# Interleaving the V rows by four over the partitions in a fused sketch-attention and feed-forward kernel, with a new hand-written order of work

## The chip, the core and the metric

One core of a Trainium2 chip runs the whole kernel. The metric is the device time of one launch in microseconds, as the median of repeated runs. A profiled execution gives, beside its own time, the span from its first to its last instruction and what each engine did in it.

The engines are named as the profile names them: PE (matrix multiply; PEld is its weight load), DVE (vector), ACT (activation functions), POOL (general vector work) and SP (which here only issues DMAs). An issue row, such as `SPq`, is the engine's sequencer starting a DMA. PSUM is the memory that PE writes, SBUF the memory that everything else works in, with 128 partitions.

## The reference

Four batches (b), four heads (h), 1088 positions (s), head size 32, sketch size 8. All tensors are float32.

```python
def phi(x):                                   # 32 -> 64 features
    a = np.einsum('rd,bhsd->bhsr', S1, x)
    b = np.einsum('rd,bhsd->bhsr', S2, x)
    return np.einsum('bhsi,bhsj->bhsij', a, b).reshape(*x.shape[:-1], r * r)
q_p, k_p = phi(q), phi(k)
kv = np.einsum('bhsf,bhsd->bhfd', k_p, v)
z = np.sum(k_p, axis=2)
num = np.einsum('bhsf,bhfd->bhsd', q_p, kv)
den = np.einsum('bhsf,bhf->bhs', q_p, z)[..., None] + 1e-06
x = (num / den).transpose(0, 2, 1, 3).reshape(4352, 128)
h = x @ w_in                                  # 128 -> 2048
out = (h * (1.0 / (1.0 + np.exp(-h)))) @ w_out   # 2048 -> 128
```

The sums over keys (`kv` and `z`) run over all 1088 positions in any order, so the key and value rows may be dealt to partitions and columns in any way, as long as a key and its value meet in the same partition of the same block of 128.

## The kernel before, in words

**Two halves.** The attention half works batch by batch. For each batch a key part makes `kv` and `z`, and a query part makes the 128 x 1088 block `xT` (features by tokens). The feed-forward half then takes `xT` in pieces of 256 or 512 tokens: `h` steps (L729, PE, w_in times x into a PSUM tile of two banks), SiLU (L733, ACT, 128x1024 elements at a time) and `o` steps (L746 or L743, PE, the sum over the 2048 hidden columns). There are 68 SiLU instructions: 16 for the whole tokens of each batch, and 4 for the tokens left over by all batches (two of each 34 per partition, task `mR`). A piece ends with a copy or transpose to an output tile `ot` (L751 on DVE, L164 or L162 for the last ones) and four stores (L701, L707, L712). The H tiles in PSUM are two, so an `h` step waits until the SiLU two steps back has read its tile. Output tiles come from a pool of 3.

**Key part of one batch** (`key_tasks`, from L294). A key or value of a head is position 34 i + a, with i from 0 to 31 and a from 0 to 33. The 34 values of a are cut into four groups c with `KA = [0, 9, 18, 26, 34]`, sizes `KN = [9, 9, 8, 8]`.
- `kt` (L301, L304): DVE transposes K in 32 x 32 blocks into `KT`, two groups c at a time. Group c goes to `KT[:, c, :]`, as 9 or 8 blocks of 32 consecutive columns. For batch 0 it is four instructions (two for each of the two parts of the load), for each later batch two, of 576 and 512 columns.
- `proj` (L268 to L274): PE, both sketches of the keys. `tr` (L321): DVE transposes the sketches back to `kab`, keys over the partitions: partition 32 c + i holds what group c has for i.
- `outer` (L324 to L327): DVE or POOL makes the 64 features per key and head, `kp`. `z` (L329), `l2`, `wm`: the denominators' weights.
- `load_v` (L188): V of group c goes to partitions 32 c to 32 c + 31, one DMA per group, 128 to 144 KB. `vcast` (L401) makes bfloat16 of it on ACT, POOL or DVE. `kv0` (batch 0, L357) and `kv` (L379): PE sums kp times V over the keys, nine blocks of 128 (the last of 64). `kvm`, `kvt`, `kvc`: copies and a transpose of the result.

**Query part.** Batch 0 (`query_tasks`, from L532) works in small spans so that the first tokens come soon: `tr` (L543, DVE), `proj`, `projm` (L558), `back` (L565), `backm` (L570), `scale` (L473 to L476), `outer` (L481), a transpose on PE (`pet`, L502) and a copy (`petc`), `num` (L515), and the copy `x` to `xT`. Batches 1 to 3 (`query_tasks_hm`, from L605) work in one piece: `tr` (L613, L615), `proj` (L621, which takes one of the two H tiles until `back1` has read it), `back` 0 to 3 (L633, L634), `scale` (L641 to L644), `outer` 0 to 2 (L649), a DMA transpose for each outer (L655), `num` (L661, L669), and `x0`, `x1`, which copy halves of `xT`. Both copies must be done before the batch's first `h` step.

**What sets the order.** Every instruction is a task with a number, in order of creation; `ORDER` (L16) is a hand-written list of these numbers, and every engine executes its tasks in that order, strictly one after the other. After the point, `74` or `2.1` names the engine where a task may run on several. `Plan.replay` (L85) goes through the list once with costs written in the code, only to deal out buffers and to decide how many filler matmuls on zeros (L872) stand between the first PE tasks; the filler count is fixed when the program is built.

The orders of the queues around the change, read from `ORDER` (`m02` is the piece of batch 0 whose tokens begin at block 2, `m14` that of batch 1 at block 4, and so on):

```
DVE  k0kt00 k0kt20 WP WB4 k0kt05 k0tr00 k0kt25 k0tr10 k0outer0 k0tr05 k0tr15 q0tr4 q0tr0 k0outer6 q0back14
     k0wm q0back10 q0back04 q0back00 q0backm00 q0backm20 q0scale20 q0outer20 q0scale00 k1kt00 k1kt20 q0backm44
     q0scale44 k1tr00 k1tr10 q0x0 q1tr q0petc4 q0petc6 k2kt00 k2kt20 q1back0 q1back1 q1back3 q1back2 q1scale
     q1outer1 q1outer0 k1outer6 k2tr00 k2tr10 q2tr k1kvm m00tr k1kvc k3kt20 k2wm q1x0 k3kt00 q2back0 ...
POOL k0outer1 k0outer3 k0outer7 k0outer5 k0vcast5 q0outer00 cwi1 cwi2 q0outer44 q0outer64 WQ k1outer8 k1outer0
     cwo0 cwo1 k1outer4 cwo3 cwi3 k1vcast k1outer2 k2outer2 q1outer2 ...
ACT  lv03 lv02 l2out lv12 k0zt k0vcast0 k0kvm q0petc2 cwi0 q0x2 lv13 q0petc0 m02s0 m02s1 ... m04s7 q1x1 m14s0 ...
PE   ... k0proj0 l2in k0proj5 k0z q0proj4 k0l2 q0proj0 q0projm0 q0projm4 k0kv0 ... k0kv3 q0pet2 q0num2 q0pet0
     m02h0 k1proj m02h1 ... m04h5 k1kv k2z m04h6 k1kvt m04h7 k2l2 q1num m04o4 m04o5 q2proj m14h0 m04o6 m04o7
     m10h0 m02o0 m10h1 k3proj q1numr m14h1 m02o1 m14h2 m02o2 m10h2 m02o3 ...
SP   lqb lqa lv00 lv01 lk1 lwi0 lwi1 lq1 lk2 lwo0 lwo1 lwo2 lv11 lwo3 lk3 lv10 lq2 q1dmat1 q1dmat0 ...
```

Names: `lk`, `lq`, `lv` are loads of K, Q and V (`lqa` and `lqb` the two parts of batch 0's Q, of 256 and 288 KB; `lv03` is group 3 of batch 0), `lwi` and `lwo` the weights' loads, `cwi` and `cwo` their casts. Batch 0's K is loaded by four DMAs on SP ahead of all this (L203 to L205). The S1 and S2 loads and four of the sixteen V loads (`lv02`, `lv03`, `lv12`, `lv13`) are issued by ACT.

Of the kernel before, what the change touches and what calls it, by code (L numbers as in the profile page):

```python
# [16 lines left out]
0 74 7 25 28 22 1 24 29 23 2.1 97 3.1 30 33 8 5 31 11 34 6 102 32 100 35 38.1 140 40.0 36 14 37 75  # L17
16 50 42.0 18 55 51 99 76 20 52 46.1 56 79 48.0 53 59 57 78 58 77 44.0 60 26.0 67 27.1 68 39 41
69.0 47 45 49 61 43 70 54.1 104 71.0 62.1 9.1 105 72 10.0 73.0 80 63 183 81 101 12.0 241 98 64.0
106 145 242 244 82.1 107 65 108 245 247 66.1 87.1 114 122 248 226 83 4 115 88 113.0 227 84.1 116  # L20
229 109.0 89.1 117.1 147 85 230 123 15.0 148 90 86.0 124 17.0 232 91.0 125 228 111.0 233 127 231
126 256 19.1 128 259 257 149 21.0 234 260 13.0 262 131.0 258 263 235 261 129.0 236 132 265 264
103.0 266 112.1 268 130 237 150 269 110.0 250 151 267 165 251 271 153.0 118 272 157 119.0 133.1 274
238 158 156.0 120 277 239 275 121.0 191 159 155.0 135 240 160.0 278 270 137.1 273 190 138.0 134 166
310 167 188 276 168 311 144 279 170 142 283 280 143 243 284 286 169 282 192 171 287 136 313 281 246
314 316 187 193 249 172.1 141 317 289 185 252 290 312 253 292 194 254 285 176.0 293 319 174.0 288
255 146.0 320 322 152.1 315 175 323 295 139.1 154.1 291 296 196.0 298 173 200 299 301 197.0 184 294
201 186 302 325 92.1 177 202 161 326 328 162.0 203.0 297 329 163 304 164.0 208 300 305 178 189.0
# [91 lines left out]
def kernel(  # L120
# [31 lines left out]
    op = ctx.enter_context(tc.tile_pool(name="op", bufs=3))  # L152
# [35 lines left out]
    def load_v(eng, b, c):  # L188
        n = KN[c]
        eng.dma_start(  # L190
            Vx[b][32 * c: 32 * (c + 1), :, 0:n].rearrange("p h a d -> p h (a d)"),
            AP(tensor=v.tensor, offset=v[b, 0].offset + KA[c] * D,
               ap=[[SA * D, 32], [S * D, H], [1, n * D]]))
# [46 lines left out]
    for t in KTs:  # L240
        nc.vector.memset(t[:, 2:4, NB * 32:], 0.0)
    for t in Vf:
        nc.vector.memset(t[64:, :, NB, :], 0.0)
# [21 lines left out]
    def dma(kb, fn, deps=(), issue=0.47, lag=1.8, due=None, ready=0.0, eng="SP", rate=300.0, name=""):  # L265
        return pl.add(eng, issue, fn, deps, lag=lag, due=due, ready=ready, dq=kb / rate, name=name)
# [9 lines left out]
    def load(b):  # L276
# [8 lines left out]
        if b >= 2:  # L285
# [4 lines left out]
        ks[b]["lv"] = [dma(139, lambda c=c: load_v(nc.scalar if b == 1 and c > 1 else nc.sync, b, c), dv, due=at + 0.5, rate=220.0,  # L290
                           eng="ACT" if b == 1 and c > 1 else "SP", name=f"lv{b}{c}") for c in range(4)]
        qs[b]["lq"] = dma(557, lq, dq, due=at + 1.0, name=f"lq{b}")

    def key_tasks(b, cuts):  # L294
# [6 lines left out]
        def kt(c, lo, hi):  # L301
            hi = min(hi, KN[c])
            src = Kx[b][:, KA[c]: KA[c + 2], :].rearrange("p (c a) d -> p c a d", c=2)[:, :, lo:hi, :]
            nc.vector.transpose(out=KT[:, c:c + 2, 32 * lo: 32 * hi], in_=src.rearrange("p c a d -> p c (a d)"))  # L304
# [24 lines left out]
        def z(sl):  # L329
            st["z"] = sl  # L330
            for t in range(NBX):
                n, c = (P if t < NB else XN), t % 4
                nc.tensor.matmul(sl[32 * c: 32 * (c + 1), 0:HR], st["ab"][:n, 1, t, :], st["ab"][:n, 0, t, :],  # L333
# [23 lines left out]
        def kv0(lo, hi):  # L357
            i = st.get("n", 0)
            kpf = st["kp"].rearrange("p (t q g) i j -> p t q (g i j)", q=2, g=2)
            for t in range(lo, hi):  # L360
                m = P if t < NB else XN
                for p in range(2):
                    nc.tensor.matmul(H0[:, p, 0:64].rearrange("p (g d) -> p g d", g=2), kpf[:m, t, p, :],
                                     Vb[b][:m, 2 * p: 2 * p + 2, t, :], start=(i == 0), stop=(i == NBX - 1))
                i += 1
# [13 lines left out]
        def kv(sl):  # L379
            st["kvp"] = sl  # L380
            kpf = st["kp"].rearrange("p (t h) i j -> p t h (i j)", h=H)
            for t in range(NBX):
                n = P if t < NB else XN
                for h in range(H):
                    nc.tensor.matmul(sl[D * h: D * (h + 1), 0: R * R], Vb[b][:n, h, t, :],
                                     kpf[:n, t, h, :], start=(t == 0), stop=(t == NB),
# [18 lines left out]
        if b == 0:  # L405
            lv = [dma(139, lambda c=c: load_v(nc.scalar if c > 1 else nc.sync, 0, c), due=5.0 + 0.1 * c, rate=230.0,
                      eng="ACT" if c > 1 else "SP", name=f"lv0{c}") for c in range(4)]
# [415 lines left out]
    ld_qa = dma(262, lambda: load_x(nc.sync, Qx[0], q, 0, 0, 16), due=4.0, rate=250.0, name="lqa")  # L823
# [81 lines left out]
```

## Time and profile before

| what | value |
|---|---|
| median of 11 runs | 99.05 us (97.02 to 101.03) |
| the profiled execution's own time | 98.15 us |
| its span, first to last instruction | 96.3 us |
| busy in the span: PE, ACT, DVE, POOL | 87.1, 72.4, 56.8, 31.6 us |
| of PE's busy time, fillers on zeros | 9.9 us (54 matmuls) |
| SiLU on ACT | 64.8 us, 68 instructions |
| first `h` step on PE | 17.48 us after the span's start |
| batch 1's first `h` step | 37.09 us |
| last `o` step ends | about 91.4 us |
| packets of DMA | 28506, 12.93 MB |

How to read it. Times in the profile count from the start of the span. In a row of the timeline the first number is the start, the second the busy time of the instructions that the row merges; the note in brackets is the engine's idle time ahead of it and what ended it. In a row of the table by stretches the engines' busy times stand in order, with their instruction counts, then the clock granted to PE, the mean busy share of 16 DMA engines and the GB/s moved. PE is busy in nine tenths of the span, but a good part of that is fillers and waiting matmuls, and its busy time is modelled at the ends of instructions; what is late at a given place is read from the row at that place.

### The profile page before, as it was taken

Reading aid. Unit: us, or ns where it says so; the run is one execution under the profiler, and the core shown is the slowest. Engines: PE = TensorE matmul, PEld = TensorE weight load, DVE = VectorE, ACT = ScalarE, POOL = GpSimd, SP = SyncE. Lnnn points to the kernel's source line nnn. Section 1 sums busy time; section 2 is a strip of 40 time slices with the busy share of each in tenths; the row PEclk is TensorE's granted clock in tenths of the full one; section 3 lists DMA queues with packets and bytes.
Section 4 is the critical chain, followed back from the end, with each engine's and each line's share of the span. In section 5 each row is a group of like instructions: output and inputs, shape, how many; then the busy total and the mean of one; then the engine's idle time right before and its main releaser. Section 6 shows DMA issues by size and latency. Waiting matters only on the chain.

```text
span 96.3 us, 2487 instructions
## 1 busy us (share of the span) xinstructions
PE 87.1 (90%) x962; PEld 51.9 (54%) x972; DVE 56.8 (59%) x153; ACT 72.4 (75%) x89; POOL 31.6 (33%) x46
## 2 busy tenths in 40 slices
PE   5999599989999789999999999999999999999900
PEld 4645359776566434465454344544565854579800
DVE  4665879599999998948607394999207022020210
ACT  3310115899999884799999689999999989999700
POOL 5019605799881390061194450053000000000000
PEclk9999859999999999999999999999999999999999
DMA  1989999999700843299878100671740433406220
GB/s 39 251 252 241 328 349 396 371 241 269 216 22 7 162 74 68 65 298 195 187 151 186 33 0 0 101 117 34 137 85 0 70 72 61 76 0 95 47 63 14
DMA packets 28506, 12.93 MB, mean 134 GB/s; under 512 B 23120, under 2 KB 26704, under 8 KB 28496
## 3 DMA queue, kind: packets, MB, share of 16 engines
q1 hardware_dynamic: 27680, 12.20, 52.8%
q10 hardware_dynamic: 816, 0.60, 2.6%
q8 instruction: 7, 0.11, 0.6%
q14 instruction: 3, 0.02, 0.1%
HBM read 8.79 MB, written 2.23 MB: 114 GB/s over the span
## 4 chain that ended last, share of the span: by engine, by line
PE 66%; DMA 15%; DVE 8%; SPq 5%; issue 2%; DVEq 0%
PE H L729 26%; PE B L746 22%; DMA Qx<-in_q_dram 7%; DMA qt<-qp 4%; PE B L872 4%; DMA out_dram<-ot 4%; SPq L701 2%; SPq L186 2%; PE B L743 2%; DVE kab L321 2%; PE B L272 1%; DVE qp L649 1%; PE H L621 1%; DVE QT L613 1%; PE B L558 1%
## 5 line engine op out<-in xcount | busy, mean ns | idle before, releaser
L733 ACT ACTIVATE G<-H 128x1024 bf16<-128x1024 f32 x68 | 64.8, 1034 | 5.3 <-PE B L621 2.3
L729 PE MATMUL H<-xT,w_in 128*128 128x512 bf16 (+1 forms) x153 | 36.9, 336 | 0.1
L746 PE MATMUL B<-G,w_out 128*128 128x512 bf16 (+1 forms) x125 | 31.4, 352 | 0.3
L729 PEld LDWEIGHTS <-w_in 128*128 128x128 bf16 x176 | 18.1, 114 | 11.3 <-issue 3.7
L746 PEld LDWEIGHTS <-w_out 128*128 128x128 bf16 x128 | 12.2, 97 | 10.2 <-issue 0.7
L327 POOL TENSOR_TENSOR kp<-kab 128x512 bf16<-128x512 f32 (+1 forms) x14 | 13.8, 1005 | 8.6 <-DVE kab L321 8.6
L751 DVE STREAM_TRANSPOSE ot<-B 128x512 f32<-128x512 f32 (+1 forms) x8 | 5.1, 641 | 11.0 <-PE B L746 11.0
L872 PE MATMUL B<-zero 128*128 128x256 bf16 x54 | 9.9, 332 | 1.1 <-DVE fmask L233 1.1
L649 POOL TENSOR_TENSOR qp<-aqs,qabm 128x1024 bf16<-128x1024 f32 (+1 forms) x3 | 4.8, 1592 | 12.7 <-DVE aqs L644 12.7
L649 DVE TENSOR_TENSOR qp<-aqs,qabm 128x1024 bf16<-128x1024 f32 (+1 forms) x6 | 8.0, 1365 | 0.1
L872 PEld LDWEIGHTS <-zero 128*128 128x128 bf16 x54 | 5.7, 116 | 3.3 <-DVE fmask L233 1.1
L304 DVE STREAM_TRANSPOSE KT<-Kx 128x576 f32<-128x576 f32 (+4 forms) x10 | 6.0, 618 | 1.7 <-DMA Kx<-in_k_dram 1.6
L743 PE MATMUL B<-w_out,G 128*128 128x128 bf16 x96 | 6.7, 219 | 0.0
L164 POOL CAST Vh<-Vf 128x1152 bf16<-128x1152 f32 (+1 forms) x4 | 4.0, 1010 | 8.1 <-DMA Vf<-in_v_dram 8.1
L743 PEld LDWEIGHTS <-G 128*128 128x128 bf16 x96 | 6.0, 98 | 0.8
L164 DVE COPY ot<-B 128x128 f32<-128x128 f32 x5 | 1.3, 287 | 7.1 <-DMA out_dram<-ot 7.1
L481 POOL TENSOR_TENSOR qp<-aqs,qabm 128x512 bf16<-128x512 f32 (+1 forms) x4 | 3.8, 958 | 3.9 <-DVE aqs L476 3.9
L164 DVE CAST xT<-B 128x512 bf16<-128x512 f32 (+1 forms) x5 | 3.0, 621 | 3.3 <-PE B L661 3.2
L327 DVE TENSOR_TENSOR kp<-kab 128x512 bf16<-128x512 f32 (+1 forms) x7 | 4.5, 646 | 0.0
L633 DVE STREAM_TRANSPOSE qabm<-H 128x256 f32<-128x256 f32 x6 | 2.6, 429 | 2.0 <-PE B L621 2.0
L613 DVE STREAM_TRANSPOSE QT<-Qx 128x1024 f32<-128x1024 f32 x3 | 3.7, 1219 | 0.0
L338 ACT ACTIVATE zt<-B 128x32 f32<-128x32 f32 x4 | 0.8, 211 | 3.1 <-PE B L333 3.1
(101 smaller groups left out, 79.2 us busy)
## 6 DMA issues: line engine op xcount, KB each, us to landing
Kx<-in_k_dram SPq DMA_DIRECT2D x3, 544.0 KB, 7.8
Qx<-in_q_dram SPq DMA_DIRECT2D x3, 544.0 KB
out_dram<-ot SPq DMA_DIRECT2D x24, 64.0 KB, 2.0
Vf<-in_v_dram SPq DMA_DIRECT2D x8, 144.0 KB, 5.5
w_inf<-in_moe_w_in_dram SPq DMA_DIRECT2D x2, 512.0 KB, 8.2
w_outf<-in_moe_w_out_dram SPq DMA_DIRECT2D x4, 256.0 KB, 10.1
out_dram<-ot SPq DMA_DIRECT2D x18, 32.0 KB, 1.6
Vf<-in_v_dram ACTq DMA_DIRECT2D x4, 128.0 KB
```

Source lines behind the costliest of these rows:

```text
L164: eng.tensor_copy(out=out, in_=in_)
L304: nc.vector.transpose(out=KT[:, c:c + 2, 32 * lo: 32 * hi], in_=src.rearrange("p c a d -> p c (a d)"))
L327: eng.tensor_tensor(out=st["kp"][:, H * lo: H * hi], in0=_bc(a, 2, R), in1=_bc(bb, 1, R), op=ALU.mult)
L481: eng.tensor_tensor(out=st[f"qp{lo}"], in0=_bc(st["aqs"][:, H * lo: H * hi], 2, R), in1=_bc(bq.rearrange("p a (h r) -> p (a h) r", h=H), 1 ...
L613: nc.vector.transpose(out=QT[:, :, 0: 32 * NB].rearrange("p c (a s) -> p a c s", s=32), in_=Qx[b][:, 0: 4 * NB, :].rearrange("p (a c) d -> ...
L649: eng.tensor_tensor(out=st["qp", i], in0=_bc(st["aqs"][:, g0: g0 + n], 2, R), in1=_bc(grp(1)[:, g0: g0 + n], 1, R), op=ALU.mult)
L729: nc.tensor.matmul(view(sl, i), w_inj[:, (J * jp + i) // 4, (J * jp + i) % 4, :], x, start=True, stop=True)
L733: nc.scalar.activation(out=sl, in_=cc[jp], func=ACT.Silu)
L743: nc.tensor.matmul(d[:, 0:P], view(cc["g", jp], i)[:, P * t: P * (t + 1)], w_out[:, j, :], start=(j == 0), stop=(j == NJ - 1))
L746: nc.tensor.matmul(cc["o"][:, :n], w_out[:, j, :], view(cc["g", jp], i), start=(j == 0), stop=(j == NJ - 1))
L751: nc.vector.transpose(out=cc["ot"][:, :n], in_=cc["o"][:, :n])
L872: nc.tensor.matmul(hold["bank"][:, 0:256], zero[:, 0:P], zero, start=True, stop=True)
```

## The change

1. `load_v`: V of group c goes to partitions c, c + 4, c + 8, ... (step 4) in place of 32 c to 32 c + 31.
2. `kt`: the transposes write K's columns in the matching order. A block of 32 transposed columns is dealt over the four column groups q of `KT`, 8 columns to each, and within a group to columns 4 s + c. An instruction of 576 columns so writes runs of 8 elements whose step is 4 elements (16 bytes), where before it wrote runs of 32 consecutive ones. Sources and sizes are the same.
3. Because groups 2 and 3 have 8 rows, the holes of the ninth block now lie in all partitions: the zeroing of `KT` and V covers all four groups and all 128 partitions, and the matmuls on the ninth block (`z`, `kv0`, `kv`) take 128 rows in place of 64.
4. All V loads are issued by SP.
5. The pool of output tiles has 5 in place of 3.
6. Some rates that only `Plan.replay` uses are other numbers.
7. `ORDER` is another list. Many tasks change place, and some their engine.

The new queues around the change:

```
DVE  k0kt00 k0kt20 WP k0kt05 k0tr10 k0kt25 k0tr00 k0outer3 k0tr15 k0tr05 q0tr0 q0tr4 q0back10 q0back00 k0wm
     q0back14 q0back04 q0backm00 q0backm20 q0scale20 q0outer20 q0scale00 k1kt00 k1kt20 q0backm44 q0scale44 k2kt00
     k1tr10 q0x0 k1tr00 q0petc4 k2kt20 q1tr k2tr00 k1wm k2tr10 cwo1 q1back0 q1back1 q1back2 q1back3 q1scale
     q1outer0 q1outer1 k2wm m02tr q2tr m00tr k3kt20 q2back0 q2back3 q2back1 q1x0 k3kt00 q2back2 q2scale ...
POOL WQ k0outer1 k0outer6 k0outer0 k0outer7 k0outer5 q0outer00 cwi2 q0outer44 q0outer64 k1outer8 k1outer6
     k1outer2 cwi3 k1outer0 cwo0 cwo2 k1vcast cwo3 k1outer4 q1outer2 q0outer84 k2outer4 ...
ACT  WB4 l2out k0zt k0vcast0 k0vcast5 cwi1 k0kvm q0petc2 cwi0 q0x2 q0petc0 m02s0 m02s1 ... m04s5 k1kvm k1kvc
     m04s6 q1x1 m04s7 m14s0 ...
PE   ... k0proj0 k0proj5 l2in k0z q0proj0 k0l2 q0proj4 q0projm0 k0kv1 k0kv3 k0kv0 k0kv5 q0projm4 k0kv7 k0kv6
     q0pet2 q0num2 q0pet0 m02h0 m02h1 k1proj q0num0 m02h2 q0pet4 m00h0 k1z q0num4 m00h1 k2proj k1l2 m00h2 q0pet6
     q1proj k2z m02h3 ... m04h5 k1kv q2proj m04o0 k1kvt m04h6 m04o1 q1num m04h7 m04o2 m04o3 m14h0 m04o4 m14h1
     q1numr k3proj m10h0 m04o5 m10h1 m04o6 m10h2 m04o7 ...
SP   lqa lqb lv01 lv02 lv00 lv03 lwi0 lk1 lwi1 lk2 lq1 lwo1 lwo2 lwo0 lv21 lv12 lv10 lv13 lv23 lv11 lwo3 lv20
     lq2 lk3 lq3 lv32 q1dmat0 q1dmat1 m02st0 m00st0 q1dmat2 ...
```

Further on, the casts of V of batches 2 and 3 (`vcast`) move from POOL to DVE, and the leftover piece `mR` moves from among the last steps of batch 2 to among those of `m30`, nearer the end. The diff, without `ORDER`:

```diff
-    op = ctx.enter_context(tc.tile_pool(name="op", bufs=3))
+    op = ctx.enter_context(tc.tile_pool(name="op", bufs=5))
...
-            Vx[b][32 * c: 32 * (c + 1), :, 0:n].rearrange("p h a d -> p h (a d)"),
+            Vx[b][c::4, :, 0:n].rearrange("p h a d -> p h (a d)"),
...
-        nc.vector.memset(t[:, 2:4, NB * 32:], 0.0)
+        nc.vector.memset(t[:, :, NB * 32:], 0.0)
     for t in Vf:
-        nc.vector.memset(t[64:, :, NB, :], 0.0)
+        nc.vector.memset(t[:, :, NB, :], 0.0)
...
-        ks[b]["lv"] = [dma(139, lambda c=c: load_v(nc.scalar if b == 1 and c > 1 else nc.sync, b, c), dv, due=at + 0.5, rate=220.0,
-                           eng="ACT" if b == 1 and c > 1 else "SP", name=f"lv{b}{c}") for c in range(4)]
+        ks[b]["lv"] = [dma(139, lambda c=c: load_v(nc.sync, b, c), dv, due=at + 0.5, name=f"lv{b}{c}") for c in range(4)]
...
-            nc.vector.transpose(out=KT[:, c:c + 2, 32 * lo: 32 * hi], in_=src.rearrange("p c a d -> p c (a d)"))
+            dst = KT.rearrange("p q (t s c) -> p c t q s", s=8, c=4)[:, c:c + 2, lo:hi]
+            nc.vector.transpose(out=dst, in_=src.rearrange("p c a d -> p c (a d)"))
...
-                n, c = (P if t < NB else XN), t % 4
-                nc.tensor.matmul(sl[32 * c: 32 * (c + 1), 0:HR], st["ab"][:n, 1, t, :], st["ab"][:n, 0, t, :],
+                c = t % 4
+                nc.tensor.matmul(sl[32 * c: 32 * (c + 1), 0:HR], st["ab"][:, 1, t, :], st["ab"][:, 0, t, :],
...
-                    nc.tensor.matmul(sl[D * h: D * (h + 1), 0: R * R], Vb[b][:n, h, t, :],
-                                     kpf[:n, t, h, :], start=(t == 0), stop=(t == NB),
+                    nc.tensor.matmul(sl[D * h: D * (h + 1), 0: R * R], Vb[b][:, h, t, :],
+                                     kpf[:, t, h, :], start=(t == 0), stop=(t == NB),
...
-            lv = [dma(139, lambda c=c: load_v(nc.scalar if c > 1 else nc.sync, 0, c), due=5.0 + 0.1 * c, rate=230.0,
-                      eng="ACT" if c > 1 else "SP", name=f"lv0{c}") for c in range(4)]
+            lv = [dma(139, lambda c=c: load_v(nc.sync, 0, c), due=5.0 + 0.1 * c, name=f"lv0{c}") for c in range(4)]
```

## The prediction

> **What bounds the kernel now.** I read the engines' shares first, then the table by stretches, then the timeline at the places where the stretches show slack.
>
> ```profile
> PE 87.1 (90%) x962; PEld 51.9 (54%) x972; DVE 56.8 (59%) x153; ACT 72.4 (75%) x89; POOL 31.6 (33%) x46
> ```
>
> The shares alone say PE. The stretches say more; the columns are PE, PEld, DVE, ACT, POOL, granted clock, DMA share, GB/s.
>
> ```profile
> 4.00:8.00 4.00, 3.77 (x54) 2.14 (x58) 3.24 (x11) 0.28 (x1) 1.12 (x1) 1.00 0.95 257
> 8.00:12.00 4.00, 2.89 (x66) 1.65 (x69) 2.59 (x9) 0.60 (x2) 3.17 (x5) 0.91 1.01 284
> ...
> 22.00:26.00 4.00, 3.95 (x63) 2.56 (x70) 3.88 (x13) 3.82 (x8) 3.71 (x6) 1.00 0.97 258
> 26.00:30.00 4.00, 4.00 (x36) 2.11 (x22) 3.88 (x4) 3.95 (x5) 2.77 (x3) 1.00 0.09 32
> 30.00:34.00 4.00, 3.14 (x67) 2.13 (x67) 4.00 (x7) 3.41 (x5) 1.10 (x2) 1.00 0.60 114
> 34.00:38.00 4.00, 3.64 (x59) 1.46 (x61) 3.46 (x11) 2.62 (x4) 2.16 (x3) 1.00 0.38 66
> ```
>
> Until 12 us the DMAs are full (share 0.95 to 1.01). From 22 to 34 us DVE is full, and from 30 to 38 PE and ACT both have holes: they wait for batch 1. After 38 us PE is busy 95% and more until about 91.4. So three stages: loads and the first attention pieces; a race of DVE against the 16 SiLUs of batch 0; then PE.
>
> ```profile
> 9.89 0.71 DVE L543 STREAM_TRANSPOSE QT<-Qx 128x512 f32<-128x512 f32 x1 [1.41 <-DMA Qx<-in_q_dram]
> ...
> 19.29 0.85 DVE L321 STREAM_TRANSPOSE kab<-B 128x288 f32<-128x288 f32 x2 [0.91 <-PE H L729]
> ...
> 28.35 3.11 DVE L649 TENSOR_TENSOR qp<-aqs,qabm 128x1024 bf16<-128x1024 f32 x2
> ...
> 37.81 1.02 ACT L733 ACTIVATE G<-H 128x1024 bf16<-128x1024 f32 x1 [1.23 <-PE B L621]
> ```
>
> DVE's two long waits (for Q, then for k1proj behind an `h` step on PE), its outers of batch 1 that end at 31.46, and the SiLU that starts batch 1 at 37.81 are the places that the change moves.
>
> **The change part by part.** The sum is made against the profiled execution, 98.15 us (span 96.3 plus 1.85 around it), 0.9 below the median of 99.05. A difference is carried to the median unchanged.
>
> V interleaved, issued by SP. In the packets of the trace V's 1152-byte packets took 75 ns in the first 12 us (246 GB/s over 16 engines), Q's of 2048 bytes 98 ns (335). V's 0.557 MB would take 2.26 us at the one rate, 1.66 at the other: between 0 and 0.6 us of transfer. This is hidden: V was cast at 11.60, `kv0` started at 14.43, and POOL's last key outer ends at 10.8, which holds `kv0` anyway. [...] Without that cover V would be worth 0.6 us. ACT loses four issues of 0.32 to 0.41 us; three come before its first SiLU, one (17.02) runs beside PE's fillers: 0. SP gains four of 0.33 to 0.47 us; its next load, `lk1`, is needed by DVE only at 14 us: 0.
>
> Q ahead of V. K, Q and V together are 1.67 MB; Q no longer shares the engines with the two V loads of ACT. At 257 GB/s 1.11 MB take 4.3 us in place of 6.5 for all: Q's last part, landed at 9.83, lands about 2 us earlier. DVE's 1.41 us wait goes; what is late next is DVE's own queue.
>
> DVE up to `scale20` (12.77 before). Out: the 1.41 wait, a 0.27 wait, WB4 0.27 (to ACT, idle there), outer0 0.43, outer6 0.57. In: outer3 0.65 to 0.78, more waits on PE for `l2` and `projm`, since `proj` now follows both transposes (about 0.7). I follow the queue with the rows' durations and get `scale20` at 11.35: 1.4 earlier. By the same queue `outer20` ends at 13.2 in place of 14.55; pet, petc, num, x then put the first `h` step at about 15.1 in place of 17.48, if the fillers, whose number the built program fixes, fit.
>
> DVE from there to `q1back0` (23.59). The 0.91 wait goes (k2kt00 fills it). Added ahead: k2tr twice 0.42, k1wm 0.12, cwo1 0.62; petc6 0.36 leaves: +1.2. So q1back0 moves by -1.4 - 0.9 + 1.2 = -1.1, and q1outer1 ends near 30.4.
>
> From there to batch 1. Before, 5.63 us passed to its first `h` step at 37.09. Now on PE `q2proj` (0.7) stands ahead of m04h6 and waits for q2tr, which on DVE follows the outers: 30.4 + k2wm 0.1 + m02tr 0.38 + q2tr 1.27 = 32.1. Queued behind it on PE are m04o0, m04h6, q1num, m04h7; ACT waits with them. h7 then needs the H tile that q2back1 frees: DVE 32.1 + m00tr 0.38 + k3kt20 0.65 + three backs 1.7 = 34.85. After h7 0.45 and two `o` steps 0.86, m14h0 starts at 36.15: -0.95. k1kvm and k1kvc on ACT (0.3 each) and k1outer6 on POOL leave that path; SP's transposes (issue 1.3, landing 3.4 as before) end by 34, before q1num can run.
>
> PE after that. When batch 1 starts, four `o` steps of batch 0 are left (m04o4 to o7) in place of six (m04o6, o7, m02o0 to o3). Two of 0.43: -0.87 of the 54.3 us that PE needs from 37.09 to 91.4. V's casts on DVE (1.15 us on POOL) fall into 42 to 66, where DVE is busy 46 to 83%: 0; without that slack 1.2 each. The tail: last `o` step to end stays 4.9 us. The pool of 5: the `ot` copies of the tail start at 89.07 and 91.46, when PE's own last step of the piece ends (88.48 + 0.61; 89.40 + 2.02), so nothing; `mR` later adds stores to SP ahead of `m30`'s, 1.9 us against 1.8 of PE between them: 0 to 0.1.
>
> Zeroing: 0.1 us more on DVE before its first transpose, which waits 0.65 for K: 0. Matmuls with 128 rows for 64: 193 ns both (L363): 0.
>
> The strided transposes. No row shows DVE writing elements 16 bytes apart. From below: L633 writes runs of 8 elements at the speed of L321's runs of 16, so nothing, and a gain has no reason since size and source are the same. From above, three zeroings on POOL:
>
> ```profile
> L246 POOL MEMSET WQ<- x2: 124/124/124, 1.5 to 1.6; 128x32 f32 x2
> ...
> L248 POOL MEMSET AW<- x2: 162/162/162, 1.6 to 1.7; 128x36 f32 x2
> ...
> L250 POOL MEMSET QT<- x2: 151/152/152, 1.7 to 1.8; 128x64 f32 x2
> ```
>
> L246 and L250 write runs (0.88 ns for each further element); L248 writes single elements 36 bytes apart and takes 34.5 ns more than 36 elements in a run: 0.96 ns each. The elements on the path to batch 1 are 256 + 192 (batch 0's second part; the first is covered by the waits for K), 1088 (k1), 1088 (k2) and 512 (k3kt20) = 3136: between 0 and 3.0 us. I take 0, because L633 and L304 are the same operation on the same engine and the zeroing is another on another. [...]
>
> Sum: -0.95 - 0.87 = -1.8, so 96.35 for the profiled execution and 97.2 for the median.
>
> **The rivals.** (a) The strided writes cost what POOL's row says. For it: L248, and DVE is the full engine from 22 to 34 us. Against: the four run lengths that cost DVE nothing. -1.8 + 3.0 = +1.2: 100.2 us. It decides from 1.8 / 3136 = 0.57 ns for each element; from 1.2 ns the kernel is over 2% slower. (b) The whole early start is carried: first `h` 2.4 earlier, and PE's holes from 30 to 38 (0.86 + 0.36) close. This needs DVE's q1 group without POOL beside it: L644 took 1.36 in batch 1 and 0.46 in batch 2, L649 1.85 and then 1.21, which is 1.5 us to win. Against: POOL now has k1outer4, q1outer2 and k2outer4 there. -2.4 - 1.2 = -3.6: 95.45. (c) The opposite: POOL beside both outers and the first product of the scale: 1.85 for 1.21 and 1.36 for 0.46 once more, +1.55. -0.25: 98.8. (d) V's new layout changes no rate: hidden, so the same 97.2.
>
> **How the numbers follow.** Forecast 0.40 (its own range 96.2 to 98.3), with (d) in it; (a) 0.27; (b) 0.18; (c) 0.15. Two per cent of the median is 2.0 us, about what a measurement of this kernel can tell from no change: below 97.05 is faster, above 101.05 slower. Faster: 0.18 of the forecast's 0.40, all of (b), 0.04 of (a) where the price is far below POOL's: 0.40. Slower: 0.15 of (a), where the price exceeds 1.2 ns or the delay repeats at batch 2, and 0.05 of (c): 0.20. Same: 0.40. The range reaches from below (b), 94.9, to (a), 100.3.
>
> **What would show it.** Right: L543 without a wait for Q; `kv0` before 12.5; first `h` near 15.1; L304 at 0.68 and 0.77 us; q1outer1 ending near 30.4; ACT idle around 31 to 33 for L621; m14h0 near 36.2; PE full after. Wrong: L304 at 1.2 us and more is (a); m14h0 before 34 is (b); L649 twice at 1.8 is (c). A first `h` still at 17 would mean that fillers or POOL hold it.

## The result, and the profile after

The changed kernel takes 99.57 us (median of 12 runs, 98.14 to 99.99) beside 98.42 us (47 runs, 96.23 to 101.39) for the kernel before in the same comparison: a ratio of 1.0206, 95% interval 1.0161 to 1.0252. By the ratio it is about 2.0 us slower (the two medians lie 1.15 us apart), where 1.8 us of gain were forecast. Ratios here compare undisturbed runs alone, so one can differ from the quotient of the medians beside it. The profiled execution took 99.54 us, its span 97.2.

The page of the changed kernel, busy time by engine:

```profile
PE 85.0 (87%) x961; PEld 50.9 (52%) x970; DVE 57.4 (59%) x148; ACT 73.9 (76%) x95; POOL 38.3 (39%) x48
```

PE has 2 us less to do than before and the span is longer: PE waits more. The stretches say where (same columns as in the prediction):

```profile
14.00:17.50 3.50, 2.41 (x29) 1.98 (x34) 2.55 (x4) 3.22 (x8) 1.26 (x2) 1.00 1.03 409
17.50:22.00 4.50, 3.48 (x57) 2.33 (x41) 4.40 (x11) 3.05 (x4) 3.24 (x4) 1.00 0.88 286
...
30.00:34.00 4.00, 2.98 (x54) 1.91 (x52) 4.00 (x6) 3.74 (x5) 4.00 (x4) 1.00 0.43 82
34.00:38.00 4.00, 3.63 (x52) 1.56 (x54) 3.77 (x12) 2.12 (x4) 1.61 (x2) 1.00 0.59 105
38.00:42.00 4.00, 3.50 (x33) 1.53 (x33) 3.86 (x9) 3.14 (x4) 0.87 (x1) 1.00 0.36 83
...
66.00:74.00 8.00, 6.51 (x39) 3.13 (x39) 2.40 (x7) 6.53 (x8) 0.00 (x0) 1.00 0.36 62
```

PE lacks 1.1 us from 14 to 17.5, 1.0 from 17.5 to 22, has the old hole from 30 to 38, and a new one from 66 to 74, where it did 6.51 us of work in 8. The kernel before was full there:

```profile
66.00:74.00 8.00, 7.95 (x57) 4.29 (x57) 3.05 (x8) 7.87 (x10) 0.00 (x0) 1.00 0.35 67
```

Three places in DVE's timeline of the changed kernel, the last two in the first two of these stretches:

```profile
7.61 1.26 DVE L540 STREAM_TRANSPOSE QT<-Qx 128x512 f32<-128x512 f32 x2
...
14.91 2.19 DVE L304 STREAM_TRANSPOSE KT<-Kx 128x576 f32<-128x576 f32 x2 [1.41 <-DMA Kx<-in_k_dram]
...
18.58 1.21 DVE L304 STREAM_TRANSPOSE KT<-Kx 128x576 f32<-128x576 f32 x1
```

The wait of 1.41 us for Q is gone, as forecast. A wait of the same 1.41 us for batch 1's K stands in its place, and each transpose of 576 columns takes 1.2 us where it took 0.77. The groups of the two pages give the second fact as a sum for the same ten instructions, 6.0 us before and 9.3 us in the changed kernel:

```profile
L304 DVE STREAM_TRANSPOSE KT<-Kx 128x576 f32<-128x576 f32 (+4 forms) x10 | 6.0, 618 | 1.7 <-DMA Kx<-in_k_dram 1.6
...
L304 DVE STREAM_TRANSPOSE KT<-Kx 128x576 f32<-128x576 f32 (+4 forms) x10 | 9.3, 963 | 2.3 <-DMA Kx<-in_k_dram 2.2
```

By shape, 576 columns went from 0.766 to 1.225 us and 512 from 0.680 to 1.104: 0.80 and 0.83 ns more for each element. SP's queue in the changed kernel says why K is late (start, busy time, and how many issues the row merges):

```profile
3.88 2.67 SPq L190 DMA_DIRECT2D Vf<-in_v_dram  x4
6.59 0.59 SPq L824 DMA_DIRECT2D w_inf<-in_moe_w_in_dram  x1
7.23 0.43 SPq L176 DMA_DIRECT2D Kx<-in_k_dram  x1
```

SP's queue before:

```profile
3.79 0.91 SPq L190 DMA_DIRECT2D Vf<-in_v_dram  x2
5.49 0.35 SPq L176 DMA_DIRECT2D Kx<-in_k_dram  x1
```

The four V loads keep SP busy for 2.67 us, 0.67 each with the gaps between them; before, batch 0's took 0.34 to 0.44 each on SP and ACT. K of batch 1 is issued at 7.23, before at 5.49, and the first quarter of `w_in` behind V too: ACT waited 2.25 us for it, until 13.56.

To compare the kernels I cut each profiled span at three places that a reader can find in any timeline: the start of batch 1's first key transpose on DVE, the start of batch 1's first SiLU on ACT (the 17th), and the end of PE's last matmul. Four legs, in us:

| kernel | to k1's transpose | to batch 1's SiLU | to PE's end | tail | span |
|---|---|---|---|---|---|
| before (profile shown above) | 15.37 | 22.44 | 53.61 | 4.84 | 96.3 |
| before, once more (e1) | 14.56 | 22.01 | 53.33 | 4.86 | 94.8 |
| changed | 14.91 | 23.93 | 53.85 | 4.48 | 97.2 |
| e3, order alone | 13.38 | 23.01 | 53.19 | 4.48 | 94.1 |
| e6, order and strided transposes | 15.33 | 23.92 | 53.66 | 4.48 | 97.4 |
| e7, order and interleaved V | 14.38 | 22.94 | 53.17 | 4.51 | 95.0 |
| e10, e3 with one DMA moved | 14.89 | 22.89 | 52.34 | 4.48 | 94.6 |
| e12, changed with that DMA moved | 14.25 | 23.93 | 52.37 | 4.51 | 95.1 |

Every leg is that of one profiled execution. The first legs of e6 and e10 are long for a reason of their own, told at the end.

### The profile page after: what moved, and what is told of

It reads as the page before. It is cut to its first block, busy times and chain, and to the rows that moved or that the text cites. A ratio compares the mean times of both kernels' runs of the same rounds, so it can differ in the third digit from the quotient of the medians.

```text
span 97.2 us, 2474 instructions
## 1 busy us (share of the span) xinstructions
PE 85.0 (87%) x961; PEld 50.9 (52%) x970; DVE 57.4 (59%) x148; ACT 73.9 (76%) x95; POOL 38.3 (39%) x48
## 4 chain that ended last, share of the span: by engine, by line
PE 49%; DMA 20%; DVE 16%; SPq 7%; issue 3%
PE H L726 21%; PE B L743 17%; DMA Kx<-in_k_dram 10%; DMA qt<-qp 9%; PE B L740 6%; DVE KT L304 5%; SPq L698 4%; DVE QT L610 2%; SPq L190 2%; DVE qp L646 2%; DVE Vh L164 2%; DVE kp L327 2%; PE H L618 1%; PE B L272 1%; DVE ot L748 1%
## 5 line engine op out<-in xcount | busy, mean ns | idle before, releaser
L327 POOL TENSOR_TENSOR kp<-kab 128x512 bf16<-128x512 f32 (+1 forms) x18 | 17.8, 1011 | 1.5 <-DVE kab L321 1.5
L646 POOL TENSOR_TENSOR qp<-aqs,qabm 128x1024 bf16<-128x1024 f32 (+1 forms) x5 | 10.0, 2016 | 14.2 <-DVE aqs L641 14.2
L304 DVE STREAM_TRANSPOSE KT<-Kx 128x576 f32<-128x576 f32 (+4 forms) x10 | 9.3, 963 | 2.3 <-DMA Kx<-in_k_dram 2.2
L869 PE MATMUL B<-zero 128*128 128x256 bf16 x52 | 8.8, 312 | 1.1 <-DVE fmask L233 1.1
L478 POOL TENSOR_TENSOR qp<-aqs,qabm 128x512 bf16<-128x512 f32 (+1 forms) x4 | 4.8, 1201 | 4.5 <-DVE aqs L473 4.5
L164 DVE CAST xT<-B 128x512 bf16<-128x512 f32 (+1 forms) x6 | 3.7, 637 | 3.8 <-PE B L658 3.8
L646 DVE TENSOR_TENSOR qp<-aqs,qabm 128x1024 bf16<-128x1024 f32 (+1 forms) x4 | 4.4, 1126 | 0.0
L618 PE MATMUL H<-QT,WQ 32*32 32x288 f32 x48 | 2.3, 412 | 1.3 <-DVE QT L612 1.3
L499 PE MATMUL B<-identb,qp 128*128 128x128 bf16 x18 | 1.8, 219 | 1.4 <-DVE kab L321 1.0
L162 ACT ACTIVATE w_in<-w_inf 128x512 bf16<-128x512 f32 x2 | 1.3, 633 | 2.2 <-DMA w_inf<-in_moe_w_in_dram 2.2
```

Of the source, the lines that this page charges most:

```text
L164: eng.tensor_copy(out=out, in_=in_)
L304: nc.vector.transpose(out=dst, in_=src.rearrange("p c a d -> p c (a d)"))
L327: eng.tensor_tensor(out=st["kp"][:, H * lo: H * hi], in0=_bc(a, 2, R), in1=_bc(bb, 1, R), op=ALU.mult)
L478: eng.tensor_tensor(out=st[f"qp{lo}"], in0=_bc(st["aqs"][:, H * lo: H * hi], 2, R), in1=_bc(bq.rearrange("p a (h r) -> p (a h) r", h=H), 1 ...
L646: eng.tensor_tensor(out=st["qp", i], in0=_bc(st["aqs"][:, g0: g0 + n], 2, R), in1=_bc(grp(1)[:, g0: g0 + n], 1, R), op=ALU.mult)
L869: nc.tensor.matmul(hold["bank"][:, 0:256], zero[:, 0:P], zero, start=True, stop=True)
```

## The experiments

All ratios are to the kernel before, run on the same chip beside the experiment.

**e1: the kernel before, once more.** No edit.

> The kernel before once more, for a profile in which PE's clock is not lowered between 11 and 14.5 us as it was in the profile shown (0.76 granted from 12 to 17.5 us). Every theory expects the same code to give a span of about 95 to 96.3 us; the prologue is the place to look: with the full clock the first h step should come before 17.48 us, by up to 1 us, since eight fillers of 0.23 us each stood ahead of kv0.

96.67 us, span 94.8. It matters because of the clock (last three columns: clock granted to PE, DMA share, GB/s). The profile that the prediction was made on:

```profile
10.00:12.00 2.00, 1.34 (x27) 0.75 (x31) 2.00 (x7) 0.40 (x1) 1.18 (x3) 0.81 1.01 341
12.00:14.00 2.00, 2.00 (x22) 1.13 (x15) 1.49 (x8) 0.33 (x1) 0.26 (x1) 0.50 1.05 349
```

And the same kernel in e1:

```profile
10.00:12.00 2.00, 1.83 (x38) 1.06 (x39) 1.97 (x10) 0.74 (x1) 1.00 (x2) 1.00 1.01 393
12.00:14.00 2.00, 1.67 (x29) 1.38 (x28) 1.76 (x7) 0.44 (x2) 0.00 (x0) 1.00 1.07 350
```

In the profiled execution PE had half its clock from 12 to 14 us. Q had also come later there, ahead of that: DVE's second transpose of it started at 9.89 us, in e1 at 9.30. In e1 the first `h` step comes at 16.20 us in place of 17.48, and the same kernel starts batch 1 at 36.57 us, not at 37.81: by this one execution, 1.24 us that the prediction took for the kernel's were that execution's.

**e2: the layout alone.** The kernel before with V interleaved and the transposes strided, and the zeroing and the matmuls of 128 rows to match; its order, engines and three output tiles kept.

```diff
-            Vx[b][32 * c: 32 * (c + 1), :, 0:n].rearrange("p h a d -> p h (a d)"),
+            Vx[b][c::4, :, 0:n].rearrange("p h a d -> p h (a d)"),
...
-            nc.vector.transpose(out=KT[:, c:c + 2, 32 * lo: 32 * hi], in_=src.rearrange("p c a d -> p c (a d)"))
+            dst = KT.rearrange("p q (t s c) -> p c t q s", s=8, c=4)[:, c:c + 2, lo:hi]
+            nc.vector.transpose(out=dst, in_=src.rearrange("p c a d -> p c (a d)"))
...
```

> The kernel before with the layout alone: V to partitions c, c+4, ..., the key transposes writing with a step of 16 bytes, zeroing and 128-row matmuls to match; old order, old issuing engines, 3 output tiles. Theory S (the strided writes are the loss): L304 takes 1.22 and 1.10 us instead of 0.77 and 0.68; 448 + 1088 + 1088 elements on the path to batch 1 at 0.8 ns make 2.1 us, so a ratio to before of about 1.02. Theory O (the new order is the loss, the layout is neutral): 1.00.

Median 99.09 us of 6 runs (96.65 to 101.48) beside 98.52 of before; too scattered for a ratio. Inconclusive on time; the transposes took 1.24 and 1.12 us here too.

**e3: the order alone.** The changed kernel with V in blocks of 32 partitions and contiguous transposes, that is with the two edits of e2 undone.

> The changed kernel with the old layout: V to 32 consecutive partitions, key transposes writing runs of 32; new order, all loads on SP, 5 output tiles kept. Theory S: L304 back at 0.77 and 0.68 us, batch 1 starts about 2.5 us earlier than in the changed kernel, ratio to before 0.99 to 1.00. Theory O: still 1.02, since the late K of batch 1, the PE wait for the query transposes and the wait for batch 3 are all still there.

97.50 us, ratio 0.9966 (0.9905 to 1.0026). The layout, then, is the loss: 0.024 of ratio lie between this and the changed kernel. But the order alone did not bring the forecast 1.8 us either. SP's queue in e3:

```profile
3.88 1.78 SPq L190 DMA_DIRECT2D Vf<-in_v_dram  x4
5.71 0.43 SPq L823 DMA_DIRECT2D w_inf<-in_moe_w_in_dram  x1
6.18 0.43 SPq L176 DMA_DIRECT2D Kx<-in_k_dram  x1
```

With V in blocks the four issues take 1.78 us and K leaves at 6.18. DVE's queue in e3:

```profile
13.38 1.37 DVE L303 STREAM_TRANSPOSE KT<-Kx 128x576 f32<-128x576 f32 x2
```

No wait for K stands in brackets, and two transposes take 1.37 us in place of 2.19.

**e6 and e7: each half of the layout by itself.** e6 undoes only V's edit, e7 only the transposes'. Keys and values no longer match in either, so only the time is read. With e3 and the changed kernel they make a square.

> The changed kernel, but V's rows lie in blocks of 32 partitions as before, while the transposes still write key columns four elements apart. Left out: keys and values no longer belong together, so only the time is read. Theory S: DVE pays about 0.8 ns for each element and the ratio is that of the changed kernel, 1.015 to 1.025, though K of batch 1 comes about 1 us earlier. Theory I (the slow issue of interleaved V and the late K are the loss): near the order alone, 0.995 to 1.003, first h step near 14.9 us. Both costs add: 1.005 to 1.015.

98.29 us, ratio 1.0074 (1.0032 to 1.0117).

> The changed kernel, but the transposes write runs of 32 columns as before, while V stays interleaved by four. Left out: keys and values no longer belong together, so only the time is read. Theory S: transposes at 0.77 and 0.68 us and the ratio of the order alone, 0.995 to 1.003. Theory I: SP's four V issues stay at 0.6 to 0.74 us each, DVE waits 1 us or more for K of batch 1, first h step at 15.4 or later, ratio 1.010 to 1.025. Both add: 1.003 to 1.012.

98.32 us, ratio 1.0121 (1.0085 to 1.0158). Against e3 the strided writes alone cost 0.011 (about 1.1 us; 0.3 to 1.8 by the two intervals taken together), the interleaved V alone 0.0155 (about 1.5 us; 0.8 to 2.2); together 0.026, and the changed kernel measures 0.024 above e3. Both suspects are guilty, and within these intervals they add.

The legs put each in its place. In the table every kernel with the new order and strided transposes needs 23.92 or 23.93 us for the second leg (so do e5 and e11 below), every one with contiguous transposes 22.89 to 23.01: the stride costs 1.0 us there. Outside the table e9 is an exception, with 13.40 and 24.91 us: there K came early, but V and `w_in` later still. From e3 to e7 that leg stays, and the first one grows from 13.38 to 14.38. DVE in e7:

```profile
14.38 1.37 DVE L303 STREAM_TRANSPOSE KT<-Kx 128x576 f32<-128x576 f32 x2 [0.95 <-DMA Kx<-in_k_dram]
```

SP in e7:

```profile
3.87 2.68 SPq L190 DMA_DIRECT2D Vf<-in_v_dram  x4
6.58 0.59 SPq L823 DMA_DIRECT2D w_inf<-in_moe_w_in_dram  x1
7.22 0.43 SPq L176 DMA_DIRECT2D Kx<-in_k_dram  x1
```

So 0.9 us more of issue on SP become 0.95 us of waiting on DVE, and in this pair of executions nearly all of it reaches the end (PE's last matmul at 90.49 in place of 89.58). It is the issue and not the transfer that makes K late: from the end of its issue K took 6.61 us to land in e3 and 6.71 in e7. And the DMA engines ran short of loads: their share (the last column but one) from 8 to 10 us in e3, then in e7:

```profile
8.00:10.00 2.00, 2.00 (x55) 1.03 (x45) 1.81 (x8) 0.20 (x1) 2.00 (x4) 1.00 1.03 251
...
8.00:10.00 2.00, 1.92 (x45) 0.94 (x44) 1.81 (x8) 1.40 (x3) 2.00 (x4) 1.00 0.58 137
```

**e8: the prices alone.** Each operation three times and alone; a part of the new code:

```diff
...
+        nc.vector.transpose(out=dst(1), in_=src)
+        nc.vector.transpose(out=dst(2), in_=src)
+        nc.vector.transpose(out=dst(3), in_=src)
+        nc.vector.transpose(out=dst(4), in_=src)
...
+            nc.sync.dma_start(Vp[32 * c: 32 * (c + 1)], vsrc(c))
...
+            nc.sync.dma_start(Vp[c::4], vsrc(c))
...
```

> Not the kernel's computation: DVE, ACT and POOL alone, each operation three times and one after the other: 128x576 float32 transposes and copies that write elements 1, 2, 3, 4, 5, 6, 8 and 9 apart, then V's loads to partitions 1, 2 and 4 apart, issued by SP and by ACT; the output is filled with copies. [...] Theory I: a load to partitions 4 apart takes SP 0.60 to 0.74 us to issue when nothing else runs, one to consecutive partitions 0.31 to 0.43; if the long issue was waiting for room in the queue, both take the same here.

Groups of e8; L53 to L59 write elements 1, 2, 3, 4, 5, 6 and 8 apart, L60 9 apart; the second number after the bar is ns of one:

```profile
L59 DVE STREAM_TRANSPOSE Z<-Kx 128x576 f32<-128x576 f32 x3 | 3.6, 1212 | 0.1
L60 DVE STREAM_TRANSPOSE Z<-Kx 128x576 f32<-128x576 f32 x3 | 3.6, 1205 | 0.1
...
L57 DVE STREAM_TRANSPOSE Z<-Kx 128x576 f32<-128x576 f32 x3 | 3.6, 1202 | 0.1
...
L56 DVE STREAM_TRANSPOSE Z<-Kx 128x576 f32<-128x576 f32 x3 | 3.6, 1191 | 0.1
L58 DVE STREAM_TRANSPOSE Z<-Kx 128x576 f32<-128x576 f32 x3 | 3.5, 1183 | 0.1
L55 DVE STREAM_TRANSPOSE Z<-Kx 128x576 f32<-128x576 f32 x3 | 2.8, 937 | 0.1
L54 DVE STREAM_TRANSPOSE Z<-Kx 128x576 f32<-128x576 f32 x3 | 2.3, 779 | 0.1
L53 DVE STREAM_TRANSPOSE Z<-Kx 128x576 f32<-128x576 f32 x3 | 2.3, 759 | 12.0 <-POOL Z L72 12.0
```

759, 779, 937, 1191, and then flat: 1202, 1183, 1212 and 1205 ns at steps of 5, 6, 8 and 9. The price rises up to a step of 4 elements (16 bytes) and not beyond. A step of 2 is nearly free (779 for 759 ns), a step of 4 pays in full (1191): 0.75 ns an element. The runs show the size of the price and not its cause. It is not DVE's alone: the copy of the same tile took ACT 682 ns with a step of 1 and 1212 with 4, POOL 668 and 1201, DVE 460 and 678.

SP in e8, four loads of V each: 32 consecutive partitions (L75), every second one (L77), every fourth (L79):

```profile
7.50 1.75 SPq L75 DMA_DIRECT2D Vf<-in_v_dram  x4
10.74 2.69 SPq L77 DMA_DIRECT2D Vf<-in_v_dram  x4
15.30 2.62 SPq L79 DMA_DIRECT2D Vf<-in_v_dram  x4
```

0.44, 0.67 and 0.66 us an issue, gaps included, with no other loads in flight than these. ACT's first issue to every fourth partition, with every load ahead of it landed, took 0.68 and 0.61 us (at 43.14 and 93.75 us), its first to consecutive ones 0.32 both times (at 60.66 and 89.34). So the long issue is not a wait for room in a queue; it is the price of partitions that are not consecutive, 0.67 us where they are 2 apart and 0.66 where they are 4 apart, for 0.44. V's packets of 1152 bytes took 64 to 70 ns on average in SP's nine groups of loads, 67 to 70 to consecutive partitions and 66 to 68 to every fourth: alone, the layout changes next to nothing in the rate of transfer.

**e4: let PE do the permutation.** The changed kernel, but DVE writes runs and the keys' projection reads its columns in the new order.

```diff
-            dst = KT.rearrange("p q (t s c) -> p c t q s", s=8, c=4)[:, c:c + 2, lo:hi]
-            nc.vector.transpose(out=dst, in_=src.rearrange("p c a d -> p c (a d)"))
+            nc.vector.transpose(out=KT[:, c:c + 2, 32 * lo: 32 * hi], in_=src.rearrange("p c a d -> p c (a d)"))
...
+            cols = KT.rearrange("p c (t q s) -> p q t s c", q=4, s=8)
...
```

> The changed kernel with V interleaved as it is, but the keys' columns are put in order by PE: the transposes write runs of 32, and the projection matmuls of the keys (L272) read their moving columns as 9 x 8 x 4 with steps of 32, 1 and 288 elements. Theory S: as e3_order_only plus V's better rate, ratio to before 0.985 to 1.00, provided that L272 on KT stays near 0.31 us for 160 columns and 0.42 for 288. If PE pays for the scattered read, those matmuls grow (by half or more) and most of the gain goes. Theory O: 1.02.

99.19 us, ratio 1.0221 (1.0146 to 1.0296). The transposes were back at 0.77 and 0.68 us, and nothing was won. A group of e4:

```profile
L309 PE MATMUL B<-KT,WP 64*32 64x288 f32 x48 | 3.5, 652 | 0.0
```

The projection's matmul, which here reads its moving columns out of order, takes 652 ns in place of the changed kernel's 414: the price moved to PE, about 0.46 us for each projection. The second leg is 23.30 us, so a part was won there; K was as late as in the changed kernel (issued at 7.22).

**e5: half of V's issues on ACT again.** The changed kernel, but the last two V loads of batches 0 and 1 are ACT's (the line for batch 1 has the same change).

```diff
...
-            lv = [dma(139, lambda c=c: load_v(nc.sync, 0, c), due=5.0 + 0.1 * c, name=f"lv0{c}") for c in range(4)]
+            lv = [dma(139, lambda c=c: load_v(nc.scalar if c > 1 else nc.sync, 0, c), due=5.0 + 0.1 * c, name=f"lv0{c}") for c in range(4)]
```

> The changed kernel, but the last two V loads of batches 0 and 1 are issued by ACT, as before the change; V stays interleaved and the transposes strided. Theory S (the strided writes on DVE are the loss): a transpose of 576 columns stays at 1.2 us and the time at the changed kernel's, ratio 1.015 to 1.025. Theory I (SP needs 0.6 to 0.74 us to issue one interleaved V load, and so K of batch 1 comes late): K's load is issued about 1.3 us earlier (near 5.9 us in place of 7.23), DVE's wait of 1.41 us for it falls to 0.5 or less, and 0.6 to 1.2 us are won: ratio 1.008 to 1.015. If the DMA engines, full until 12 us, set K's arrival and not the issue, the wait stays above 1 us and the ratio is that of S.

98.94 us, ratio 1.0176 (1.0136 to 1.0216); not told apart from the changed kernel. K was issued at 5.93 and DVE did not wait for it, but V's last part now came late, its cast started at 12.80 in place of 10.05, so one late load was exchanged for another. Besides, this execution was slow at the start for a reason of its own (told at the end), so its first leg can't be read.

**e9: K ahead of V.** The changed kernel, with the load of batch 1's K moved ahead of the four V loads on SP.

```diff
         self.replay(seq)
+        names = [t["name"] for t, c in seq]
+        it = seq.pop(names.index("lk1"))
+        names.remove("lk1")
+        seq.insert(names.index("lv01"), it)
```

> The changed kernel, but SP issues the load of batch 1's K ahead of batch 0's four V loads; nothing else moves. Theory L (the interleaved V loads cost what they delay: K of batch 1, for which DVE waits 1.41 us): K is issued near 3.9 us in place of 7.23, the wait goes, V lands some 2 us later, near 12 us, which the weights' arrival at 13.56 covers, and about 1 us is won: ratio 1.007 to 1.014. Theory W (what is delayed to effect is w_in, for which ACT waits 2.25 us and which stays where it is): the wait of DVE goes, but the first h step stays at 16 and the ratio at 1.016 to 1.025. If V itself becomes late, the cast on ACT starts after 13 us, the first h step moves behind 16.5 and the kernel is slower than the changed one.

99.11 us, ratio 1.0169 (1.0091 to 1.0248): as the changed kernel, within its interval. DVE's transposes started at 13.40 without a wait, 1.5 us earlier, and it did not help. V was cast at 11.29 (10.05) and `w_in` at 14.46 (13.56). The stretches of e9:

```profile
10.00:12.00 2.00, 0.77 (x12) 0.41 (x5) 1.70 (x8) 0.71 (x2) 0.95 (x2) 1.00 0.77 267
12.00:14.00 2.00, 1.92 (x28) 1.34 (x28) 1.90 (x6) 0.55 (x2) 0.43 (x1) 0.52 0.98 342
14.00:17.50 3.50, 3.50 (x31) 2.91 (x29) 3.36 (x8) 2.76 (x7) 1.24 (x2) 0.79 1.02 408
```

PE waited for V from 10 to 12 us (0.77 busy of 2.00), and was then granted 0.52 and 0.79 of its clock. That clock may have cost a part of what the early K won: of e9's six runs the one with a mean granted clock of 1.00 took 98.10 us, the other five, at 0.97 to 0.99, took 98.62 to 100.78. My theory that the late K is the one thing that costs fell here in part: SP's extra issue time delays all that stands behind it, and to put one load first only chooses which. All three, K, V and `w_in`, are wanted before 14 us.

**e10 and e12: the wait from 66 to 74 us.** In the changed kernel PE waits there for batch 3's queries. PE's timeline:

```profile
69.57 0.41 PE L658 MATMUL B<-qt,KVd 64*32 64x512 bf16 x8 [1.44 <-DMA qt<-qp]
```

SP in the same place:

```profile
59.36 1.27 SPq L652 DMA_TRANSPOSE qt<-qp  x1
60.94 3.08 SPq L698 DMA_DIRECT2D out_dram<-ot  x6
64.55 1.24 SPq L652 DMA_TRANSPOSE qt<-qp  x1
```

POOL had written that product at 61.25, and its DMA transpose was issued at 64.55, behind six issues of stores. e10 is e3, e12 the changed kernel, each with this edit alone:

```diff
         self.replay(seq)
+        names = [t["name"] for t, c in seq]
+        it = seq.pop(names.index("q3dmat0"))
+        names.remove("q3dmat0")
+        seq.insert(names.index("q3outer0") + 1, it)
```

> The new order with V in blocks and contiguous transposes, and in it one DMA moved: SP issues the transpose of batch 3's first query product as soon as POOL has written it, ahead of three stores of batch 1. If the place in SP's queue is what makes PE wait (1.33 us before q3's numerators), the issue moves from 61.5 to about 58.3 us, the wait goes and 0.8 to 1.3 us are won: ratio 0.984 to 0.990. If the DMA engines, full at that time, set the landing, the wait shrinks by less than 0.5 us and the ratio stays at 0.993 to 1.001.

> The changed kernel as it is, V interleaved and transposes strided, with the one DMA moved that e10 moved: batch 3's first query product is transposed ahead of three stores. If the wait for it is a cost of the new order that has nothing to do with the layout, PE's 1.44 us wait goes, PE is busy 7.8 of the 8 us from 66 to 74, and the ratio falls by about the same 0.012 as with the old layout, from 1.0206 to 1.005 to 1.012. If the layout's delays make something else late there, the ratio stays above 1.015.

e10: 96.12 us, ratio 0.9844 (0.9780 to 0.9907), faster than both kernels. e12: 97.95 us, ratio 1.0109 (1.0051 to 1.0168). Both gained what the first theory expected of them, 0.012 and 0.010 of ratio. SP in e12:

```profile
58.66 3.14 SPq L656 DMA_TRANSPOSE qt<-qp  x2
61.89 5.34 SPq L702 DMA_DIRECT2D out_dram<-ot  x8
```

The stretch of e12, where the changed kernel's PE did 6.51 us:

```profile
66.00:74.00 8.00, 8.00 (x46) 3.57 (x44) 2.46 (x5) 7.86 (x9) 0.00 (x0) 1.00 0.23 40
```

The third leg is 52.34 and 52.37 us, 0.8 to 1.5 below that of e3 and the changed kernel. (In e5's profile PE did not wait there, though the issue was as late, at 64.55: the transpose landed at 67.69, in the changed kernel at 69.53. So it is the landing that decides, and it varies; with the early issue PE did not wait in either profile.) The distance from e10 to e12 is the layout's price a second time: 0.0265, beside 0.024 from e3 to the changed kernel.

**e11: three output tiles.** The changed kernel with `bufs=3` in the `op` pool.

> The changed kernel with three output tiles in place of five. If the two added tiles do nothing (the prediction's 0), the ratio stays within 0.004 of the changed kernel's 1.0206. If the new order's stores need them, an output copy waits for a store, in 60 to 70 us or in the tail, and the ratio rises to 1.025 or more.

99.38 us, ratio 1.0202 (1.0153 to 1.0251), with the changed kernel's 1.0206: the two added tiles do nothing here.

## Why the prediction was wrong, point by point

The sum was -0.95 (start of batch 1) and -0.87 (PE after it). Measured from the first profile of before, batch 1's first SiLU is 1.03 later and PE's leg after it 0.24 longer.

- **The strided transposes: "took 0".** The step that failed, and rival (a). 0.80 ns for each element in the kernel, 0.75 alone, against bounds of 0 and 0.96 from POOL's zeroing. POOL's row, on another engine and another operation, was the better one because it alone was of single elements apart (36 bytes); L633's runs of 8 consecutive elements (407 to 451 ns for 256 columns) and L321's of 16 (435 to 482 for 288) say nothing on elements 16 bytes apart, which alone on DVE took 1191 ns for 759 (e8). On the forecast's 3136 elements this is 2.5 us of DVE time. Some 1.0 of it reaches batch 1 in the second leg, and the ratios (0.011 of 98 us) say about as much for the end. Of the rest, k3kt20's 0.42 us cost 0.1, since DVE waited for PE there anyway (0.20 in e3). Rival (a)'s sum of +1.2 us came nearest, and that is luck: its mechanism is there, but 1.0 of its 3.0 us reached the end, the -1.8 it starts from came as -0.3 (e3), and V's issue, which it had not, cost 1.5 (e7). (The 1.85 us of L649 in (b) and (c) is a mean over four; batch 1's first took 1.98.)
- **V's issue on SP: "four of 0.33 to 0.47 us ... needed by DVE only at 14 us: 0".** Failed too, and nobody's rival. An issue to partitions 4 apart takes 0.60 to 0.74 us, K of batch 1 is needed at 13.4 once DVE is early (e3), and it landed behind that, at 14.89. Nor is K the next load: the first quarter of `w_in` stands between, and ACT waited for it. It cost 1.0 us of first leg and 0.0155 of ratio (e7 against e3). The row that was used is the row of an issue with another shape of access: I carried a duration over to a form that the trace did not show, without a bound.
- **"PE full after."** Failed. The forecast moved by name the transposes of batch 1 on SP and not those of batch 3, which the new order puts behind three stores: 0.010 to 0.012 of ratio (e10, e12). Without that wait the leg is 52.35 us: 1.26 below the first profile of before and 0.98 below e1, where -0.87 was forecast. This fits the two fewer `o` steps. With that DMA moved and the old layout (e10) the whole gains 0.0156 of ratio, about 1.5 us, near the 1.8 forecast, but made up otherwise: against e1 some 0.2 at batch 1's start (e3; 0.95 forecast), 1.0 in the leg after it and 0.4 in the tail, where none was forecast.
- **The base.** The early gain of 1.4 us at `scale20` was counted from an execution in which Q came 0.59 us later than in e1 and PE had half its clock from 12 to 14 us: `scale20` started at 12.77 there, in e1 at 11.97. Against e1 the order alone is 1.18 us earlier at k1's transpose, gives back 1.0 on the way to batch 1 (the added `k2` work and `cwo1`, +1.2 in the prediction's own count), and starts it 0.18 earlier. The forecast of the place itself held: batch 1's first SiLU was due at 36.86 (37.81 less 0.95) and came at 36.39 in e3; `q1outer1` was due at 30.4 and ended at 30.03.
- **Q ahead of V: right.** No wait for Q in any kernel with the new order; `scale20` started at 10.73 (forecast 11.35). "What is late next is DVE's own queue" was right for e3 and wrong for the changed kernel, where K was.
- **First `h` near 15.1:** 14.90 in e3, 16.01 in the changed kernel, where ACT's wait for `w_in`, until 13.56, stands ahead of it (in e3 `w_in` was there at 11.87).
- **V's transfer: right, and hidden.** Packets of 1152 bytes went from 75 to 64 ns in the kernel, and `kv0` started at 10.84 (11.32 in e3, 14.43 before); the time was not in it. Alone (e8) the layout makes next to no difference, so what ran beside them probably made the 75 (with V in blocks in the new order, e3, it was 71); no run shows what.
- **Pool of 5: 0, right** (e11). **Tail: 4.9 forecast, 4.5 measured** in every kernel with the new order; not pursued. Rival (c), POOL beside DVE's products, is not seen as a loss: the group from the scale to the last outer of batch 1 took 5.8 us in the changed kernel and 6.05 in e1. Rival (b) did not come: the early start was not carried past DVE.

How the stride's time adds up: in the second leg four strided transposes of batches 1 and 2 take 1.75 us more (e7 to e12), and DVE is 1.14 later when they are through. The next instruction starts 0.16 to 0.17 us ahead of a strided transpose's end, and 0.07 to 0.08 ahead of a contiguous one's, so from start to start the four cost 1.38; of that, a product behind them (L469 in e7, L474 in e12) gives back 0.12 and a shorter wait for PE 0.11. Batch 0's four strided transposes, which the forecast's 3136 elements include in part, cost next to nothing: `scale20` started at 10.73 in the changed kernel and at 10.68 in e3, by this one pair of executions. What stays open is why e9, with K early, won nothing that can be told from noise, and why the landing of batch 3's transpose varies.

## What to carry to other kernels

The layout had a price on each side that touched it, and different engines paid: DVE, which wrote elements 16 bytes apart (1191 ns for 759, e8), SP, which issued loads to partitions 4 apart (0.66 us for 0.44, e8), and PE in place of DVE, when it read the columns out of order (652 ns for 414, e4). Before a layout is changed, each side is to be priced by a row of that very shape or measured alone, for a row of another shape was no bound here (0.33 to 0.47 us were forecast for an issue that took 0.60 to 0.74). When loads are bunched in one queue, list all that stands behind them and when each is wanted, not only the next one. And go through every piece that a new order puts behind others in a store queue, up to the last batch: the one DMA in the wrong place here was worth half of what the layout lost.

## What the runs showed of the hardware

- Writes of float32 with a step (e8): a transpose of 128x576 on DVE took 759 ns with a step of 1, 779 with 2, 937 with 3, 1191 with 4, 1183 to 1212 with 5, 6, 8 and 9. ACT's and POOL's copies of the same size nearly doubled at a step of 4 (682 to 1212, 668 to 1201), DVE's grew by half (460 to 678), read or written (672 with a read step of 4).
- The issue of a DMA of 128 rows of 1152 bytes on SP (e8): 0.44 us to consecutive partitions, 0.67 to partitions 2 apart, 0.66 to partitions 4 apart.
- PE's moving read of float32 columns out of order: 652 ns (e4) for 414 (the changed kernel), a matmul of 64x288.
- In e9 PE was busy 0.77 of the 2 us from 10 to 12 and was granted 0.52 of its clock in the next 2. In e3 it was busy 1.35 of the same 2 us and kept all of it; in the first profile of before it was busy 1.34 of them and was granted 0.50 in the next 2. No run shows what lowers the clock.
- The column of the granted clock shows 1.00 also for time of which the trace has no record. The first record stands at 3.7 to 5.4 us in ten of the thirteen profiles of this kernel's variants, at 9.1 in e10 and at 10.2 in e5 and e6. Ahead of it PE is slow: in every profile the fillers from 1.2 to 3.4 us start 0.21 us apart, and behind it, at the full clock, 0.11. So in e5, e6 and e10 PE came to its full clock 4 to 6 us later than in the others. PE in e5:

```profile
5.51 1.89 PE L869 MATMUL B<-zero 128*128 128x256 bf16 x8
```

PE in the changed kernel:

```profile
5.39 1.05 PE L869 MATMUL B<-zero 128*128 128x256 bf16 x8
```

The same eight instructions took 1.89 and 1.05 us. e10 differs from e3 only past 58 us, and its first leg is 1.51 us longer. The two later legs are free of it, which is why the legs were cut there.
